# An RWKV attention with two feed-forwards on one core: the second feed-forward's weights split into device memory ahead of time, and all diagonal fills on ScalarE

## The chip, the core and the metric

The kernel runs on one core of a Trainium2 chip. Its engines work side by side, each through a list of its own, and wait for each other by semaphores: TensorE (matrix products into PSUM), VectorE, ScalarE, GpSimd, and SyncE, whose queue issues the transfers. The profile calls them PE, DVE, ACT, POOL and SP. The metric is the device time of one run in microseconds (us); lower is better.

## The reference

Three stages follow each other: a linear attention with a decaying state over 768 positions (4 batches, 8 heads of 48 channels), a feed-forward of 384 to 768 channels that takes the largest of three products, and a gated feed-forward of 384 to 1536 channels. All of it is in 32-bit floats.

```python
for t in range(S):
    cur = np.einsum('bhd,bhe->bhde', u[None] * kt, vt)
    y[:, :, t] = np.einsum('bhd,bhde->bhe', rt, state + cur)
    state = w[None, :, :, None] * state + np.einsum('bhd,bhe->bhde', kt, vt)
...
h = np.maximum(np.maximum(x @ w1, x @ w2), x @ w3)
x = h @ w_out
...
g = x @ w_gate
out = (g / (1 + np.exp(-g)) * (x @ w_val)) @ w_out
```

## The kernel before

**Units and blocks.** The 768 positions are cut into 6 blocks of 128. A block of one batch is a unit, so there are 24 units, four to a block. A unit loads its keys and queries (`qk`, 448 KB, L259) and its natural-order keys, values and receptances (`nat`, 576 KB, L260). GpSimd scales them: `qk` twice at L266, `nat` at L270, L271 and L275; for units 0 to 3 VectorE shares this work. TensorE forms the scores `s` (L297). VectorE sums the bonus `a0` (L280). The tile `am` gets the bonus on its diagonals by eight fills of 128x128 (`fill`, L286 on VectorE or L288 on ScalarE). Of units 0 to 2 each engine fills four; the later units are ScalarE's. VectorE then copies the scores into `am` under a mask (`select`, L300). TensorE multiplies for the unit's result `y` (L317 with the state, or L322, and L326 with `am`), and for the state's growth `u` (L345). ScalarE evacuates `y` into the block's `xr` (L334), GpSimd decays the state (L352), VectorE adds `u` (L359).

**First feed-forward.** Block i has six steps f. Each makes three products `m` (nine matmuls each), whose largest becomes `h`: ScalarE copies the first out of PSUM (L398), VectorE takes two maxima (L401). ScalarE rounds `h` to a high part (L405), GpSimd makes the low part (L408). Products `o` with the second weights follow. The units of block i+1 are done between the first steps of block i, so that TensorE's order alternates between some `m`, a unit's scores, more `m`, and the unit's result.

**Second feed-forward.** Block i has twelve steps: two products `g` each, a gate of both (ScalarE L426, VectorE L429), its split (L433, L408), and three accumulating products `oo`. The results leave by L445.

**Products and weights.** Each product of two 32-bit matrices is three matmuls of halves: high by high (L384), high by low (L385), low by high (L386). The weights arrive as 64-bit numbers, 384 KB for 128x384 of them. One such third of a weight tile is a job `k`; 18 jobs make the first up-projections (`w_a`), 6 its output (`w_b`) and 36 the second feed-forward (`w_c`). A job is a fetch (L191), a scaling on ScalarE (`t`, L196), three operations on VectorE in `top` (L213, L217, L210) and two in `rest` (L225, L227), the rounding to the high half on ScalarE (`put_hi`, L230), a conversion on ScalarE (`to_float`, L234), and a product for the low half (`put_lo`, L238) on GpSimd or VectorE. The 36 jobs of `w_c` write straight into their tiles. The first four of these tiles lie in memory that the attention uses until it is done, the others reuse tiles of the first feed-forward.

**What sets the order.** The kernel is planned as it is built. `Plan.run` knows every step with its engine, an assumed cost and what it needs, and always takes the step with the lowest rank: its earliest start less 0.08 times the length of what hangs on it. TensorE's order is written out by hand and given to the plan as `tensor_order`. Each engine then works through its own list in the order in which the plan placed the steps. The products `m`, `o` and `g` share four PSUM banks.

## Time and profile before

| what | value |
|---|---|
| median of three runs (lowest, highest) | 910.39 us (909.04, 910.5) |
| profiled execution, its span | 909.89 us, 908.2 us |
| PE busy | 865.2 us, 95% |
| DVE busy | 383.5 us, 42% |
| ACT busy | 323.4 us, 36% |
| POOL busy | 365.3 us, 40% |
| moved by DMA | 55.45 MB |

The shares are averages over the whole span. The busy time by stretch tells more: it is given for windows of the span, with the mean clock that TensorE was granted (1.00 is full) and the busy share of the DMA engines. In a timeline each row is one instruction, or several in a row of the same kind, with its start, its duration, its engine, line and tiles, and in brackets the time that its engine idled before it and what ended the wait. Rows of groups give the busy time of all instructions of one line and kind, and the mean duration of one in ns.

### The profile page before, as it was taken

What the parts mean: (1) busy time and instruction counts of PE and PEld (TensorE: products, weight loads), DVE (VectorE), ACT (ScalarE), POOL (GpSimd) and SP (SyncE); (2) the same over time, 40 slices, a digit from 0 to 9 for tenths busy, and PEclk for the clock granted to TensorE, in tenths of its full rate; (3) what the DMA queues carried; (4) which work ended last, traced back from release to release, by engine and by line L of the source; (5) the groups of instructions that cost most, each with busy time, mean ns of one, the idle gap of its engine ahead of it and who ended that gap; (6) DMA issues with size and microseconds to landing.
All of it is one profiled execution on the core that took longest, in us unless ns stands there. A gap on an engine that the chain in (4) does not pass through costs nothing.

```text
span 908.2 us, 12109 instructions
## 1 busy us (share of the span) xinstructions
PE 865.2 (95%) x4754; PEld 703.6 (77%) x4754; DVE 383.5 (42%) x615; ACT 323.4 (36%) x675; POOL 365.3 (40%) x322
## 2 busy tenths in 40 slices
PE   7869789999999999999998799999999999999998
PEld 6647668887887887888876578888888888888886
DVE  8999973333323322448999941121012012112101
ACT  3645644342242333325655542122222113122211
POOL 7575666644546635214444442222221222122221
PEclk8889889999999999999999999999999999999999
DMA  8335432323303302012434300000000000000000
GB/s 264 117 100 184 147 125 67 89 75 94 102 1 93 102 1 93 10 36 70 123 106 122 102 36 1 1 35 1 1 1 35 0 1 35 1 1 35 1 1 35
DMA packets 19323, 55.45 MB, mean 61 GB/s; under 512 B 2400, under 2 KB 3296, under 8 KB 19264
## 3 DMA queue, kind: packets, MB, share of 16 engines
q1 hardware_dynamic: 19264, 54.67, 19.6%
q8 instruction: 37, 0.61, 0.3%
q14 instruction: 22, 0.18, 0.1%
HBM read 48.96 MB, written 4.72 MB: 59 GB/s over the span
## 4 chain that ended last, share of the span: by engine, by line
PE 73%; DVE 17%; issue 3%; ACT 1%; DMA 1%; POOL 0%; DVEq 0%; ACTq 0%; POOLq 0%
PE g L386 9%; PE g L385 9%; PE g L384 9%; PE m L384 7%; PE m L386 6%; PE m L385 6%; PE oo L385 5%; PE oo L386 5%; PE oo L384 5%; DVE t L217 4%; DVE raw L225 3%; DVE t L213 2%; DVE raw L210 2%; PE o L386 2%; PE o L384 2%
## 5 line engine op out<-in xcount | busy, mean ns | idle before, releaser
L408 POOL TENSOR_TENSOR gs<-mm,gs 128x512 fp32r<-128x512 f32 x72 | 93.7, 1302 | 287.0 <-ACT gs L433 286.5
L384 PE MATMUL g<-xhi,w_c 128*128 128x512 f32 x432 | 169.5, 392 | 9.7 <-DVE mm L429 9.3
L429 DVE TENSOR_TENSOR mm<-mm,g 128x512 f32<-128x512 f32 x72 | 49.4, 687 | 300.2 <-PE g L386 299.1
L386 PE MATMUL g<-xhi,w_c 128*128 128x512 f32 x432 | 169.3, 392 | 0.9 <-POOL w_c L238 0.8
L385 PE MATMUL g<-xlo,w_c 128*128 128x512 f32 x432 | 168.7, 391 | 0.0
L384 PE MATMUL m<-xhi,w_a 128*128 128x512 f32 x324 | 133.5, 412 | 4.7 <-DVE h L401 4.7
L386 PE MATMUL m<-xhi,w_a 128*128 128x512 f32 x324 | 129.2, 399 | 2.6 <-DVE w_a L238 2.6
L385 PE MATMUL m<-xlo,w_a 128*128 128x512 f32 x324 | 128.7, 397 | 2.3 <-POOL xlo L379 1.4
L401 DVE TENSOR_TENSOR h<-h,m 128x512 f32<-128x512 f32 x72 | 49.3, 685 | 135.7 <-PE m L386 101.2
L384 PEld LDWEIGHTS g<-xhi,w_c 128*128 128x128 f32 x432 | 81.3, 188 | 29.8 <-DVE mm L429 6.1
L408 POOL TENSOR_TENSOR hs<-h,hs 128x512 fp32r<-128x512 f32 x36 | 54.7, 1519 | 103.3 <-ACT hs L405 103.2
L386 PEld LDWEIGHTS g<-xhi,w_c 128*128 128x128 f32 x432 | 81.4, 188 | 18.8 <-POOL w_c L238 1.9
L385 PEld LDWEIGHTS g<-xlo,w_c 128*128 128x128 f32 x432 | 81.4, 188 | 16.8
L433 ACT CAST gs<-mm 128x512 fp32r<-128x512 f32 x72 | 44.6, 620 | 139.3 <-DVE mm L429 139.3
L426 ACT ACTIVATE mm<-g 128x512 f32<-128x512 f32 x72 | 43.0, 597 | 136.9 <-PE g L386 136.9
L384 PE MATMUL oo<-gs,w_c 128*128 128x512 f32 x216 | 85.8, 397 | 0.7 <-ACT gs L433 0.7
L385 PE MATMUL oo<-gs,w_c 128*128 128x512 f32 x216 | 85.3, 395 | 0.9 <-POOL gs L408 0.9
L386 PE MATMUL oo<-gs,w_c 128*128 128x512 f32 x216 | 85.1, 394 | 0.0
L384 PEld LDWEIGHTS m<-xhi,w_a 128*128 128x128 f32 x324 | 62.2, 192 | 21.1 <-ACT w_b L230 3.3
L386 PEld LDWEIGHTS m<-xhi,w_a 128*128 128x128 f32 x324 | 62.2, 192 | 17.3 <-DVE w_a L238 3.5
L385 PEld LDWEIGHTS m<-xlo,w_a 128*128 128x128 f32 x324 | 62.4, 193 | 14.9 <-POOL xlo L379 1.7
L266 POOL TENSOR_TENSOR qk<-qk,P 112x512 f32<-112x512 f32 x43 | 57.0, 1343 | 26.9 <-DMA qk<-in_qk 26.9
(107 smaller groups left out, 1243.7 us busy)
## 6 DMA issues: line engine op xcount, KB each, us to landing
raw<-in_wup SPq DMA_DIRECT2D x54, 384.0 KB, 3.2
nat<-in_nat SPq DMA_DIRECT2D x22, 576.0 KB, 5.1
qk<-in_qk SPq DMA_DIRECT2D x24, 448.0 KB, 4.4
out<-ob SPq DMA_DIRECT2D x18, 256.0 KB, 2.1
raw<-in_wout SPq DMA_DIRECT2D x6, 384.0 KB, 3.3
xr<-xr SPq DMA_DIRECT2D x10, 96.0 KB, 3.0
kv<-in_nat SPq DMA_DIRECT2D x4, 192.0 KB, 9.5
r<-in_nat SPq DMA_DIRECT2D x2, 192.0 KB, 8.2
```

Source lines behind the costliest of these rows:

```text
L210: nc.vector.tensor_scalar(out=o, in0=hw, scalar1=0x1FF, scalar2=15, op0=ALU.bitwise_and, op1=ALU.logical_shift_left)
L217: nc.vector.scalar_tensor_tensor(out=t, in0=hw, scalar=0x80000000, in1=t, op0=ALU.bitwise_and, op1=ALU.bitwise_or)
L225: nc.vector.scalar_tensor_tensor(out=lw, in0=lw, scalar=17, in1=mid if k < nearly else hw, op0=ALU.logical_shift_right, op1=ALU.bitwise_or)
L266: eng.tensor_tensor(out=a, in0=a, in1=P[0:112], op=ALU.mult)
L384: nc.tensor.matmul(p, wh_, xh, start=first, stop=False)
L385: nc.tensor.matmul(p, wh_, xl, start=False, stop=False)
L386: nc.tensor.matmul(p, wl_, xh, start=False, stop=last)
L401: nc.vector.tensor_tensor(out=hs[i, f], in0=hs[i, f], in1=banks["m", i, f, j], op=ALU.max)
L408: eng.tensor_tensor(out=g[:, 1], in0=m, in1=g[:, 0].bitcast(F32), op=ALU.subtract)
L426: nc.scalar.activation(out=hs[i, f], in_=banks["g", i, f, 0], func=AF.Silu)
L429: nc.vector.tensor_tensor(out=hs[i, f], in0=hs[i, f], in1=banks["g", i, f, 1], op=ALU.mult)
L433: nc.scalar.copy(hsplit[i, f][:, 0], hs[i, f])
```

## The change

The second feed-forward's 36 jobs no longer write their halves into the tiles from which TensorE reads. Each splits its third in place, in a scratch tile with room for both halves, and a transfer (`put_away`) writes this to a tensor in device memory, `aside`. They are paced: job n of the 36 may be fetched only after a product `m` of block 1 + n // 9 of the first feed-forward, nine jobs to each of the blocks 1 to 4. In the plan's ranking these steps no longer count by what hangs on them, but by the head of TensorE's remaining order less 15 (`behind`). Twelve transfers of 1.18 MB (`bring`) then fetch the finished tiles back: five when the attention is closed, which now includes that all 36 jobs have been put away, the others as tiles of the first feed-forward come free. The pool for raw weights moves into the attention's part of the memory, and the pool for early tiles holds five instead of four. The fills of units 0 to 3 have only ScalarE to go to. The diff, cut to its core:

```diff
+EARLY = 5
...
-    def add(self, key, on, needs, do, lag=0.0, at=0.0):
+        self.behind = {}
+    def add(self, key, on, needs, do, lag=0.0, at=0.0, behind=None):
         self.steps[key] = (on, list(needs), do, lag, at)
+        if behind is not None:
+            self.behind[key] = behind
...
+        coming = self.tensor_order[::-1]
         while ready:
             best = None
+            while coming[-1] in done and len(coming) > 1:
+                coming.pop()
+            head = coming[-1]
             for k, options in ready.items():
                 for e, t in options:
                     start, cost = max(t, free[e]), steps[k][0][e]
                     shy = self.SPARE if e == "dve" and len(options) > 1 else 0.0
-                    rank = (start + shy - self.LOOK * rest[k], start + cost)
+                    weight = rest[k] if k not in self.behind else rest[head] - self.behind[k]
+                    rank = (start + shy - self.LOOK * weight, start + cost)
                     if best is None or rank < best[0]:
                         best = rank, k, e, start, cost
...
-    raw_p = pool(ctx, "raw", bufs=2)
...
+    raw_p = pool(att, "raw", bufs=2, side="right")
...
-    weights, raws, ts = {}, {}, {}
+    weights, raws, ts, parts = {}, {}, {}, {}
+    far = pool(ctx, "far", space=bass.MemoryType.DRAM)
+    aside = [far.tile([128, 2, 3, 384], F32, name=f"aside_{f}") for f in range(NF2)]
...
     def scale(k):
-        ts[k] = raw_p.tile([128, 384], U32, tag="t", name=f"t_{k}")
+        parts[k] = raw_p.tile([128, 2, 384], U32, tag="t", name=f"t_{k}")
+        ts[k] = parts[k][:, 0]
         nc.scalar.mul(ts[k].bitcast(F32), raws[k][:, :, 1].bitcast(F32), 2.0**-112)
     def part(k, q):
         key, z, _ = jobs[k]
+        if key[0] == "c":
+            return parts[k][:, q].bitcast(F32R)
         if key not in weights:
-            where = late["wp2"] if key[0] == "c" and key[1] < 4 else wpool
-            weights[key] = where.tile([128, 2, 3, 384], F32R, tag="w", name=f"w_{key[0]}{key[1]}")
+            weights[key] = wpool.tile([128, 2, 3, 384], F32R, tag="w", name=f"w_{key[0]}{key[1]}")
         return weights[key][:, q, z]
+    def put_away(k):
+        (_, f), z, _ = jobs[k]
+        nc.sync.dma_start(out=aside[f][:, :, z], in_=parts.pop(k).bitcast(F32))
+    def bring(f):
+        t = weights["c", f] = (late["wp2"] if f < EARLY else wpool).tile([128, 2, 3, 384], F32R, tag="w", name=f"w_c{f}")
+        nc.sync.dma_start(out=t.bitcast(F32), in_=aside[f])
...
             att.close()
-            late["wp2"] = pool(ctx, "wp2", bufs=4, side="right")
...
         for k, (key, z, _) in enumerate(jobs):
+            own, pace = {}, []
+            if key[0] == "c":
+                n = k - nearly
+                own, pace = {"behind": 15.0}, [("m", 1 + n // 9, 2 * (n % 9) // 3, 2 * (n % 9) % 3)]
             if k < 4:
                 add(("fetch", k), {"none": 0.0}, [], lambda e: None, at=17.5 + 1.1 * k)
             else:
-                add(("fetch", k), {"sync": 0.5}, [("lo", k - 4), ("branch",)], lambda e, k=k: fetch(k), lag=3.0)
-            room = []
+                add(("fetch", k), {"sync": 0.5}, [("lo", k - 4), ("branch",)] + pace, lambda e, k=k: fetch(k), lag=3.0, **own)
+            add(("scale", k), {"act": 0.42}, [("fetch", k)] + ([("hi", k - 2), ("rest", k - 2)] if k > 1 else [])
+                + ([("put", k - 2)] if k - 2 >= nearly else []),
+                lambda e, k=k: scale(k), **own)
+            add(("top", k), {"dve": 1.02 if k < nearly else 1.2}, [("scale", k)] + ([("rest", k - 1)] if k else []),
+                lambda e, k=k: top(k), **own)
+            add(("rest", k), {"dve": 0.74 if k < nearly else 0.86}, [("top", k)], lambda e, k=k: rest(k), **own)
+            add(("hi", k), {"act": 0.42}, [("top", k), ("rest", k)], lambda e, k=k: put_hi(k), **own)
+            add(("float", k), {"act": 0.42}, [("rest", k)], lambda e, k=k: to_float(k), **own)
+            add(("lo", k), {"pool": 1.14, "dve": 0.5}, [("float", k), ("hi", k)], lambda e, k=k: put_lo(k, engine[e]), **own)
             if key[0] == "c":
-                f = key[1] - 4
-                room = [("attention closed",)] if f < 0 else [("m", NB - 1, f, 2)] if f < NF1 else [("o", NB - 1, NK - 1, f - NF1)]
-            add(("scale", k), {"act": 0.42}, [("fetch", k)] + ([("hi", k - 2), ("rest", k - 2)] if k > 1 else []),
-                lambda e, k=k: scale(k))
-            add(("top", k), {"dve": 1.02 if k < nearly else 1.2}, [("scale", k)] + ([("rest", k - 1)] if k else []), lambda e, k=k: top(k))
-            add(("rest", k), {"dve": 0.74 if k < nearly else 0.86}, [("top", k)], lambda e, k=k: rest(k))
-            add(("hi", k), {"act": 0.42}, [("top", k), ("rest", k)] + room, lambda e, k=k: put_hi(k))
-            add(("float", k), {"act": 0.42}, [("rest", k)], lambda e, k=k: to_float(k))
-            add(("lo", k), {"pool": 1.14, "dve": 0.5}, [("float", k), ("hi", k)], lambda e, k=k: put_lo(k, engine[e]))
+                add(("put", k), {"sync": 0.5}, [("lo", k), ("hi", k)], lambda e, k=k: put_away(k), lag=3.0, **own)
+        for f in range(NF2):
+            q = f - EARLY
+            room = ("attention closed",) if q < 0 else ("m", NB - 1, q, 2) if q < NF1 else ("o", NB - 1, NK - 1, q - NF1)
+            add(("bring", f), {"sync": 0.5}, [room] + [("put", nearly + 3 * f + z) for z in range(3)],
+                lambda e, f=f: bring(f), lag=5.0)
         def weight(k):
-            return [("hi", k), ("lo", k)]
+            return [("bring", (k - nearly) // 3)] if k >= nearly else [("hi", k), ("lo", k)]
...
-                add(("fill", n, x), {"act": 1.2, "dve": 0.75} if first else {"act": 1.2}, [("a0", n)],
+                add(("fill", n, x), {"act": 1.2}, [("a0", n)],
                     lambda e, n=n, x=x: fill(n, x, engine[e]))
...
         add(("branch",), {"none": 0.0}, rows0 + [("flag",), ("u", B - 1)]
             + [("fill", n, x) for n in range(B) for x in range(2)], branch)
         add(("attention closed",), {"none": 0.0}, [("row", NB * B - 1), ("u", NB * B - 1)]
-            + [("update", n) for n in range((NB - 2) * B, (NB - 1) * B)], attention_closed)
+            + [("update", n) for n in range((NB - 2) * B, (NB - 1) * B)] + [("put", k) for k in range(nearly, len(jobs))],
+            attention_closed)
```

The lines of the new program stand 14 to 35 further down: L236, L240, L233, L248 and L250 are the five VectorE operations of a job, L303 is the bonus sum, L323 the select, L424 the maximum, L382 the state's sum, L311 the fill, L421 the copy of `h`, L428 its rounding, L357 the evacuation of `y`, L209, L253 and L257 the scaling, the rounding and the conversion of a job.

VectorE in block 2, from the select of unit 13 to that of unit 14 (`am_13` and `am_14` are the units' tiles, `h_2_2` the third step's maximum). Before:

```order
L300 COPY_PREDICATED am_13_1998<-mask_129,s0_13_2150 128x512
L300 COPY_PREDICATED am_13_1998<-mask_129,s1_13_2151 128x512
L280 TENSOR_REDUCE a0_14_2216<-nat_14_2135 128x8
L359 TENSOR_TENSOR st_1_132<-st_1_132,u_13_2196 112x192
L401 TENSOR_TENSOR h_2_2_2245<-h_2_2_2245,m_2_2_1_2205 128x512
L401 TENSOR_TENSOR h_2_2_2245<-h_2_2_2245,m_2_2_2_2233 128x512
L300 COPY_PREDICATED am_14_2217<-mask_129,s0_14_2247 128x512
L300 COPY_PREDICATED am_14_2217<-mask_129,s1_14_2248 128x512
```

After:

```order
L323 COPY_PREDICATED am_13_2126<-mask_143,s0_13_2302 128x512
L323 COPY_PREDICATED am_13_2126<-mask_143,s1_13_2303 128x512
L236 TENSOR_SCALAR t_35_2347<-t_35_2347 128x384
L240 SCALAR_TENSOR_TENSOR t_35_2347<-raw_35_2300,t_35_2347 128x384
L233 TENSOR_SCALAR raw_35_2300<-raw_35_2300 128x384
L248 SCALAR_TENSOR_TENSOR raw_35_2300<-raw_35_2300 128x384
L250 TENSOR_SCALAR raw_35_2300<-t_35_2347 128x384
L303 TENSOR_REDUCE a0_14_2379<-nat_14_2277 128x8
L382 TENSOR_TENSOR st_1_146<-st_1_146,u_13_2358 112x192
L424 TENSOR_TENSOR h_2_2_2408<-h_2_2_2408,m_2_2_1_2368 128x512
L424 TENSOR_TENSOR h_2_2_2408<-h_2_2_2408,m_2_2_2_2396 128x512
L323 COPY_PREDICATED am_14_2380<-mask_143,s0_14_2410 128x512
```

Job 35 now stands between the select of unit 13 and the bonus sum of unit 14; the other rows keep their order.

ScalarE at the same place, from the rounding `hs_2_1` of the second step's maximum past the fills of unit 14. Before:

```order
L405 CAST hs_2_1_2172<-h_2_1_2110 128x512
L334 COPY xr_3_2131<-y_13_2176 112x4x128
L288 ACTIVATE am_14_2217<-aeye_130,a0_14_2216 128x128 x8
L398 COPY h_2_2_2245<-m_2_2_0_2161 128x512
L405 CAST hs_2_2_2270<-h_2_2_2245 128x512
```

After:

```order
L428 CAST hs_2_1_2325<-h_2_1_2244 128x512
L209 ACTIVATE t_35_2347<-raw_35_2300 128x384
L253 CAST t_35_2347<-t_35_2347 128x384
L357 COPY xr_3_2273<-y_13_2329 112x4x128
L311 ACTIVATE am_14_2380<-aeye_144,a0_14_2379 128x128 x8
L421 COPY h_2_2_2408<-m_2_2_0_2314 128x512
```

The scaling and the rounding of job 35 now stand ahead of the evacuation of unit 13's `y` and of unit 14's fills.

VectorE at the start, from unit 0's bonus sum to the select of unit 1 (`nat_1` is unit 1's natural-order load, `qk_2` and `qk_3` the keys of units 2 and 3). Before:

```order
L280 TENSOR_REDUCE a0_0_221<-nat_0_101 128x8
L286 TENSOR_SCALAR am_0_222<-aeye_130,a0_0_221 128x128 x4
L300 COPY_PREDICATED am_0_222<-mask_129,s1_0_210 128x512
L300 COPY_PREDICATED am_0_222<-mask_129,s0_0_209 128x512
L266 TENSOR_TENSOR qk_2_109<-qk_2_109,P_159 112x512
L280 TENSOR_REDUCE a0_1_269<-nat_1_106 128x8
L286 TENSOR_SCALAR am_1_270<-aeye_130,a0_1_269 128x128 x4
L300 COPY_PREDICATED am_1_270<-mask_129,s1_1_243 128x512
L300 COPY_PREDICATED am_1_270<-mask_129,s0_1_242 128x512
```

After:

```order
L303 TENSOR_REDUCE a0_0_235<-nat_0_115 128x8
L293 TENSOR_TENSOR nat_1_120<-nat_1_120 128x384
L294 TENSOR_TENSOR nat_1_120<-nat_1_120,ub_111 128x384
L323 COPY_PREDICATED am_0_236<-mask_143,s0_0_223 128x512
L303 TENSOR_REDUCE a0_1_269<-nat_1_120 128x8
L323 COPY_PREDICATED am_0_236<-mask_143,s1_0_224 128x512
L289 TENSOR_TENSOR qk_2_123<-qk_2_123,P_173 112x512
L323 COPY_PREDICATED am_1_270<-mask_143,s0_1_252 128x512
L289 TENSOR_TENSOR qk_3_129<-qk_3_129,P_173 112x512
L323 COPY_PREDICATED am_1_270<-mask_143,s1_1_253 128x512
```

The fills are gone, the two products on `nat_1` have come over from GpSimd, and the scaling of unit 3's keys has moved up.

## Rows read from the trace of the kernel before

**Rows 1.** Busy us by stretch: start:end, length, PE, PEld, DVE, ACT, POOL, clock, DMA, GB/s

```profile
59.00:97.00 38.00, 28.33 (x207) 21.58 (x207) 36.63 (x55) 22.43 (x55) 24.98 (x23) 0.86 0.44 139
...
200.40:265.50 65.10, 65.10 (x473) 52.84 (x472) 21.52 (x31) 21.97 (x54) 34.60 (x31) 1.00 0.23 69
393.90:442.80 48.90, 48.90 (x217) 40.53 (x216) 36.63 (x60) 24.00 (x49) 18.88 (x17) 1.00 0.28 76
442.80:537.00 94.20, 82.09 (x325) 63.27 (x324) 84.49 (x141) 53.28 (x106) 44.20 (x39) 0.95 0.33 95
...
537.00:610.40 73.40, 73.40 (x325) 60.79 (x324) 11.31 (x16) 17.47 (x29) 16.70 (x13) 1.00 0.03 11
```

**Rows 2.** Timeline of the start: VectorE's and ScalarE's fills (start, length, instruction)

```profile
12.42 3.74 DVE L286 TENSOR_SCALAR am<-aeye,a 128x128 f32<-128x128 f32 x4
...
17.50 1.31 DVE L266 TENSOR_TENSOR qk<-qk,P 112x512 f32<-112x512 f32 x1
...
19.31 2.79 DVE L286 TENSOR_SCALAR am<-aeye,a 128x128 f32<-128x128 f32 x4
...
25.90 1.68 DVE L286 TENSOR_SCALAR am<-aeye,a 128x128 f32<-128x128 f32 x4
...
28.58 2.45 ACT L288 ACTIVATE am<-aeye,a 128x128 f32<-128x128 f32 x8 [0.80 <-DVE a L280]
```

**Rows 3.** Timeline of one unit step in block 2, engine by engine

```profile
215.99 2.53 POOL L266 TENSOR_TENSOR qk<-qk,P 112x512 f32<-112x512 f32 x2 [4.32 <-DMA qk<-in_qk]
...
222.24 1.00 POOL L275 TENSOR_TENSOR nat<-nat,PT 128x384 f32<-128x384 f32 x1
...
217.97 1.37 DVE L300 COPY_PREDICATED am<-mask,s 128x512 f32<-128x512 uint8 x2 [0.40 <-PE s L297]
...
225.73 0.69 DVE L401 TENSOR_TENSOR h<-h,m 128x512 f32<-128x512 f32 x1 [2.57 <-ACT h L398]
...
228.12 1.36 DVE L300 COPY_PREDICATED am<-mask,s 128x512 f32<-128x512 uint8 x2 [0.40 <-PE s L297]
...
222.29 0.59 ACT L334 COPY xr<-y 112x512 f32<-112x512 f32 x1 [4.07 <-PE y L326]
222.77 2.46 ACT L288 ACTIVATE am<-aeye,a 128x128 f32<-128x128 f32 x8
...
231.30 1.09 PE L326 MATMUL y<-am,nat 128*64 128x128 f32 x16
```

**Rows 4.** Groups of VectorE by line, 59 to 97 us (busy, mean ns, idle before)

```profile
L225 DVE SCALAR_TENSOR_TENSOR raw<-raw,x 128x384 uint32<-128x384 uint32 x8 | 6.7, 836 | 0.0
L217 DVE SCALAR_TENSOR_TENSOR t<-raw,t 128x384 uint32<-128x384 uint32 x7 | 6.5, 934 | 0.0
L227 DVE TENSOR_SCALAR raw<-t 128x384 uint32<-128x384 uint32 x8 | 6.3, 793 | 0.0
L213 DVE TENSOR_SCALAR t<-t 128x384 uint32<-128x384 uint32 x7 | 5.0, 709 | 1.4 <-ACT t L196 1.4
L210 DVE TENSOR_SCALAR x<-raw 128x384 uint32<-128x384 uint32 x7 | 4.7, 669 | 0.0
```

**Rows 5.** The same view, 200 to 393 us

```profile
L225 DVE SCALAR_TENSOR_TENSOR raw<-raw 128x384 uint32<-128x384 uint32 x2 | 1.1, 560 | 0.1
...
L210 DVE TENSOR_SCALAR raw<-raw 128x384 uint32<-128x384 uint32 x2 | 0.7, 362 | 0.1
```

**Rows 6.** Timeline of VectorE beside GpSimd in block 0

```profile
60.03 1.44 DVE L227 TENSOR_SCALAR raw<-t 128x384 uint32<-128x384 uint32 x1
...
59.65 2.95 POOL L266 TENSOR_TENSOR qk<-qk,P 112x512 f32<-112x512 f32 x2
```

**Rows 7.** Transfers: 137 to 330 us, then the first 22 us (count, size, us to landing)

```profile
qk<-in_qk SPq DMA_DIRECT2D x12, 448.0 KB, 3.9
...
DMA packets 2523, 5.98 MB, mean 272 GB/s; under 512 B 412, under 2 KB 1308, under 8 KB 2522
...
qk<-in_qk SPq DMA_DIRECT2D x4, 448.0 KB, 8.8
```

More of the change, by code (lines that the diff above doesn't have):

```diff
@@ L546, in attention_closed @@
             att.close()
-            late["wp2"] = pool(ctx, "wp2", bufs=4, side="right")
+            late["wp2"] = pool(ctx, "wp2", bufs=EARLY, side="right")
         order = [(q, n) for q, n in zip("ssyuyussyuyu", (0, 1, 0, 0, 1, 1, 2, 3, 2, 2, 3, 3))]
```

## The prediction

> **What bounds the kernel now.** I read the busy time by stretch first [rows 1], since the page's shares are averages over very different stages. The reader should see three things in it. From 59 to 97 us, inside the first block of the first feed-forward, VectorE is busy for 36.63 of 38.00 us and TensorE for 28.33: VectorE, which splits the first weights, sets the pace there. In the block from 200.40 to 265.50 TensorE is busy for all 65.10 us and VectorE for 21.52: TensorE sets the pace, at a granted clock of 1.00. The block from 442.80 to 537.00 is the first of the second feed-forward. It takes 94.20 us, and the next one, with the same 325 matmuls, takes 73.40. In the long one VectorE is busy for 84.49 us, because it splits that phase's weights one step ahead of their use.
>
> Of its extra 20.80 us, 8.69 are TensorE's own (82.09 busy against 73.40, at a granted clock of 0.95), and the other 12.11 are waits. So a microsecond of waiting here came with another 0.7 us of slower matmuls.
>
> **What the change takes away.** With the splits of the 36 jobs moved forward, the block from 442.80 should run like the one after it: 94.20 - 73.40 = **20.80 us less**. What is next late there would be the weights' way back. Five tiles of 1.18 MB are asked for as the last block of the first feed-forward begins, and that block lasts 48.90 us [rows 1]. At the 272 GB/s that the queue moved in the first 22 us [rows 7] they take 5.9 / 0.272 = 22 us, so they fit, and the later tiles are each wanted one step of about 6 us (73.40 / 12) after another. I put their cost at nothing. If they got half that rate the five would take 43 us, which still fits.
>
> **The head.** VectorE's twelve fills go, in groups of four that took 3.74, 2.79 and 1.68 us [rows 2], each beside four on ScalarE. After the change ScalarE does all eight of a unit, which took it 2.45 us for unit 3 [rows 2]. By size alone that is 1.29 + 0.34 - 0.77 = 0.9 us sooner. VectorE can also do the next unit's scaling and sums, 1.81 us from 17.50 to 19.31 [rows 2], while ScalarE fills; once or twice that is hidden, so 2.7 or 4.5 us. Against it, two products of unit 1 come over from GpSimd's list, and TensorE's warm-up matmuls stand ahead of the first result. The ends are 0 and 4.5; I take **2.8 us less**, near the case of one overlap. The gain is kept, because block 0 is bound by VectorE, whose list there keeps its order.
>
> **What comes in: nine split jobs in each of blocks 1 to 4.** In volume everything fits under TensorE. A job is five VectorE operations: two of two inputs at 0.56 us and three of one at 0.36 when nothing disturbs them [rows 5], so 2.2 us, and nine add 20 us to 21.52 of 65.10. GpSimd gets at most nine products of about 1 us on 34.60. ScalarE gets three operations per job. What matters is therefore the order, and how long one job really holds VectorE.
>
> The loop to watch is this one [rows 3]. A select ends at 217.97 + 1.37 = 219.34. In the new order a whole job follows it on VectorE, and ScalarE's list has the rounding of that job ahead of the evacuation of the unit's result and of the next unit's fills. So the fill now starts no sooner than 219.34 + J + 2 x 0.48 us (the evacuation held up the fill by 0.48, and I charge the rounding the same). From the fill to the first maximum 2.96 us pass (222.77 to 225.73), two maxima take 1.38, the select 1.36. Loop: J + 6.66 us. The units follow each other every 10.15 us (217.97 to 228.12), and TensorE wants the selected tile at 231.30, 1.82 us after the select's end. Two steps of each block run through the whole loop (units 13 to 14 and 14 to 15 in this block), so TensorE is held for 2 x (J + 6.66 - 10.15) - 1.82 = **2J - 8.8 us** per block. Up to J = 4.4 this costs nothing. The step before them has two jobs but no fill in its way, and I count it as fitting.
>
> How long is J? The lower end is 2.2 us. In the stretch 59 to 97 the five operations averaged 0.84, 0.93, 0.79, 0.71 and 0.67 us [rows 4], together 3.94, with GpSimd busy for 24.98 of 38.00 us [rows 1], a share of 0.66. In the unit steps of blocks 1 to 3 its share is higher: it works without a gap from 215.99, where the next unit's keys are scaled, to the end of its last product at 223.24 [rows 3]. What such a run does to VectorE stands in [rows 6]: GpSimd's pair of products from 59.65 lasts 2.95 us (2.53 in the steady block), and beside it VectorE's one-input operation of 60.03 takes 1.44 us instead of 0.36. It starts during one GpSimd operation and ends only after it, at 61.47, 0.35 us after half of the pair. So a job that starts at 219.34 gets one operation through per GpSimd operation until about 224.0 (223.24, and 0.2 us for each of four lengthened operations), and its last one after that: J of about 5.5 us by count, and 6.9 if every operation took 1.4. The row with a comparable share says 3.94. I take 5.2, nearer to the count, since the placement right behind the select puts the job under that run.
>
> The Trainium skill speaks to this row: its page "SBUF — State Buffer", section "Who interferes with whom", says that VectorE (in its two-port modes, or with two inputs from SBUF) and GpSimd share one pair of ports as an exclusive lock, and that whoever starts first keeps it for a whole instruction. The row at 60.03 agrees, but an average of 3.94 over 38 us shows that a job is not always caught. By the rule alone this change would move 36 jobs from a stretch where GpSimd is half idle under one where it is not; the second rival below works that out.
>
> At J = 5.2 the loop costs 1.6 us per block. After the block's last select two jobs stand ahead of the maxima of the fifth step, which free TensorE's banks. They take about 5.2 + 3 us, against some 7 that TensorE can go on with the banks it has, so I add 1.3. That makes 2.9 us in each of three blocks and about 1 in the fourth, where GpSimd has only two units left to prepare: 9.6 us. TensorE's slower matmuls after a wait come on top. By the first block of the second feed-forward they are 0.7 per us, and nothing if the waits stay short; I take half: 3.4. Together **13 us more**, with ends of 0 (J up to 4.4) and about 37 (J = 6.7, by the same sum: 4.6 and 2.1 per block, 3.3 blocks, times 1.7).
>
> **Transfers and queues.** Loads of the units land after 3.9 us for the keys in the steady blocks [rows 7]. The jobs add 28 MB in blocks 1 to 4, some 109 GB/s over 258 us to the 69 of [rows 1], together well under the 272 of the start. On the queue of SyncE the write of one job waits for GpSimd's last product of it and stands ahead of a later unit's loads; that product should be done some 6 us before those loads can be asked for. A new wait is that of a job's scaling on ScalarE: its scratch tile must have been written out by the transfer of two jobs earlier, and in the step shown this scaling stands ahead of the rounding, the evacuation and the fills. That transfer is issued behind the unit's two loads, whose first lands at 215.99 [rows 3] and so left about 3.9 us earlier [rows 7], at 212.1. Put at 213.5, and at the 3.9 us of that somewhat larger load, the transfer is done by 217.4, and the scaling is due before the select's end at 219.34, so about 2 us are spare. Cost: nothing, with the rival of late transfers for the case that either isn't so.
>
> **The sum.** The profiled execution took 909.89 us. 909.89 - 20.80 - 2.8 + 13 = 899.3. The median of the runs shown, 910.39, is 0.5 longer, so I give **900 us**.
>
> **Rivals.**
> The jobs fit: J stays at 2.2 to 4.4, as the average of [rows 4] says, and TensorE never waits. 909.89 - 20.80 - 2.8 + 0.5 = 887 us, 886 to 891 with the ends of the head. For it speaks that GpSimd stops whenever TensorE does, so the run of operations doesn't last. Against it is the place of the job. Chance 0.30.
>
> The loop takes over as the bound, and the kernel is slower than before: every operation of a job is held as in [rows 6], J is 6.7 and the waits of 2 us and more bring the slower clock with them. 37 us more than nothing: 924 us, from 912 to 930. It decides against the change once the added waits exceed 20.80 + 2.8 = 23.6 us, which by the sum above is at J of about 6.2. The rule of the page "SBUF — State Buffer" of the Trainium skill would lead here. For this rival speak [rows 6], against it [rows 4]. Chance 0.18.
>
> Transfers come late: the keys took 8.8 us to land in the busy first 22 us [rows 7], 4.9 more than in the blocks. If the new traffic did half of that, the 2 us to spare ahead of the scaling would just do; if it did all of it, some 2 us at each of the 9 or 10 places where a job stands ahead of fills come on top of the forecast's 13: about 918, from 912 to 922. Chance 0.05.
>
> The weights come back late, or the last write does, so that part of the 20.80 us stays: half of it gives 910, no change. Chance 0.04.
>
> **Chances and range.** Forecast (891 to 908) 0.43, and the rivals as above. Leaving out about 0.05 below and 0.13 above, the range is 886 to 914. A measurement of this kernel can tell about 0.2%, 1.8 us, from no change. Faster: 0.43 + 0.30, less a little for the forecast's upper end, 0.71. Same: 0.08. Slower: 0.21.
>
> **What would show it.** In the changed kernel's trace: the first block of the second feed-forward lasts 73 to 74 us with TensorE busy throughout; the first up-projection starts about 3 us sooner; in blocks 1 to 3 TensorE waits for VectorE's selects and maxima, 2 to 4 us per block, with J between 4.5 and 5.5 behind the selects, and granted clocks slightly below 1.00. If J is under 4.4 there and TensorE is always busy, the first rival is right. If blocks 1 to 3 last over 73 us, the second is. If TensorE or GpSimd waits for a load, the third is. I am wrong altogether if the block after 442 us keeps its length.

## The result: 921.18 us, 1.2% slower

The changed kernel takes 921.18 us (median of 4 runs, 918.67 to 921.67) against 909.71 us before (4 runs). The ratio is 1.0123, with a 95% interval of 1.0098 to 1.0147: slower, and outside the range that was given.

The stretches of the changed kernel, cut where TensorE starts a new block (columns as in [rows 1]): block 0 of the first feed-forward, its blocks 1 to 5, and the first block of the second.

```profile
31.60:134.28 102.68, 79.46 (x475) 60.33 (x474) 88.40 (x145) 54.65 (x124) 65.80 (x57) 0.88 0.48 148
134.28:209.54 75.26, 69.86 (x474) 55.27 (x473) 55.07 (x72) 34.38 (x85) 50.31 (x44) 0.95 0.41 133
209.54:284.28 74.74, 69.84 (x474) 55.18 (x473) 57.62 (x78) 34.22 (x82) 45.54 (x39) 0.95 0.47 154
284.28:357.66 73.38, 68.20 (x473) 53.94 (x472) 57.38 (x77) 32.44 (x79) 43.22 (x38) 0.98 0.49 157
357.66:425.42 67.76, 65.27 (x409) 51.80 (x408) 48.30 (x74) 34.33 (x79) 30.25 (x27) 0.97 0.43 140
425.42:474.38 48.96, 48.96 (x217) 40.54 (x216) 12.51 (x19) 11.64 (x21) 10.28 (x8) 1.00 0.76 306
474.38:548.00 73.62, 73.62 (x326) 60.98 (x325) 11.33 (x15) 18.75 (x30) 16.69 (x13) 1.00 0.00 1
```

The last row stands where [rows 1] has 94.20 us: it takes 73.62 now, with TensorE busy throughout at a granted clock of 1.00. So the change does what it is for, and takes 20.6 us away. The four rows in the middle are the price. Before, these blocks took 65.10, 65.09, 65.10 and 63.28 us; now they take 75.26, 74.74, 73.38 and 67.76, together 32.6 us more. Block 5 is as it was (48.96), at 306 GB/s of weights coming back. The kernel before, blocks 1, 3 and 4 (block 2 is in [rows 1]):

```profile
135.31:200.41 65.10, 65.10 (x474) 52.84 (x472) 22.73 (x34) 26.44 (x70) 41.92 (x39) 1.00 0.26 81
...
265.50:330.60 65.10, 65.10 (x474) 52.84 (x473) 20.66 (x31) 22.07 (x54) 34.68 (x31) 1.00 0.23 68
330.60:393.88 63.28, 63.28 (x410) 50.56 (x409) 23.27 (x35) 18.40 (x40) 21.32 (x17) 1.00 0.12 37
```

Each of the four rows holds two losses, as the prediction's first part showed for [rows 1]. Length less PE busy is the waits: 5.4, 4.9, 5.2 and 2.5 us, together 18.0. PE busy less the old length of the block is the same matmuls at a lower clock: 4.8, 4.8, 3.1 and 2.0, together 14.6. The granted clock is 0.95 to 0.98 where it was 1.00.

What TensorE waits for there, the three largest (us in total, times, longest):

```profile
PE y L349 <- ACT hs L428: 9.2, 7, 2.2
PE o L408 <- POOL hs L431: 5.1, 3, 1.9
PE y L349 <- DVE am L323: 1.8, 7, 0.3
```

The releasers are ScalarE, GpSimd and VectorE by turns, so this view alone names no culprit. The step that the prediction followed, two units later in the trace, does. VectorE, ScalarE, GpSimd and TensorE in block 2, from the select of unit 13:

```profile
227.09 1.36 DVE L323 COPY_PREDICATED am<-mask,s 128x512 f32<-128x512 uint8 x2 [0.40 <-PE s L320]
229.94 0.74 DVE L236 TENSOR_SCALAR t<-t 128x384 uint32<-128x384 uint32 x1 [1.48 <-ACT t L209]
230.71 1.51 DVE L240 SCALAR_TENSOR_TENSOR t<-raw,t 128x384 uint32<-128x384 uint32 x1
232.26 1.53 DVE L233 TENSOR_SCALAR raw<-raw 128x384 uint32<-128x384 uint32 x1
233.82 0.56 DVE L248 SCALAR_TENSOR_TENSOR raw<-raw 128x384 uint32<-128x384 uint32 x1
234.41 0.36 DVE L250 TENSOR_SCALAR raw<-t 128x384 uint32<-128x384 uint32 x1
234.69 0.55 DVE L303 TENSOR_REDUCE a<-nat 128x8 f32<-128x384 f32 x1
...
238.66 1.48 DVE L424 TENSOR_TENSOR h<-h,m 128x512 f32<-128x512 f32 x2 [3.16 <-ACT h L421]
240.06 1.34 DVE L323 COPY_PREDICATED am<-mask,s 128x512 f32<-128x512 uint8 x2
...
229.36 0.55 ACT L209 ACTIVATE t<-raw 128x384 f32<-128x384 f32 x1 [2.01 <-DMA raw<-in_wup]
...
235.71 2.45 ACT L311 ACTIVATE am<-aeye,a 128x128 f32<-128x128 f32 x8
...
230.42 1.39 POOL L431 TENSOR_TENSOR hs<-h,hs 128x512 fp32r<-128x512 f32 x1
...
232.56 1.02 POOL L298 TENSOR_TENSOR nat<-nat,PT 128x384 f32<-128x384 f32 x1
...
253.27 0.40 PE L349 MATMUL y<-am,nat 128*64 128x128 f32 x2 [1.63 <-ACT hs L428]
```

The select ends at 228.45. The job (five rows, 229.94 to 234.77) comes before the bonus sum at 234.69, the sum before the fills at 235.71, the fills before the maxima at 238.66, these before the select at 240.06: the loop that [rows 3] closed in 10.15 us takes 12.97. The next turn takes 12.38 (240.06 to 252.44), and at 253.27 TensorE has waited for 1.63 us. The row names ScalarE's `hs`, but `y` needs the unit's two selects and not `hs`. They run from 252.44 at 0.67 us each, so the first is through at about 253.1; the rest of `y` then waits another 0.25 us, which the profile does put down to the select. The two-input operation of 230.71 takes 1.51 us and the one-input one of 232.26 1.53, where [rows 5] has 0.56 and 0.36. Their ends, 232.22 and 233.79, lie 0.41 and 0.21 us behind the ends of GpSimd's `hs` (231.81) and of its last product on `nat` (233.58). With GpSimd through, the next two take 0.56 and 0.36.

The same five operations over blocks 1 to 4, with two other groups of VectorE (busy, mean ns):

```profile
L240 DVE SCALAR_TENSOR_TENSOR t<-raw,t 128x384 uint32<-128x384 uint32 x34 | 32.5, 957 | 1.2
L233 DVE TENSOR_SCALAR raw<-raw 128x384 uint32<-128x384 uint32 x34 | 29.4, 866 | 1.2
L248 DVE SCALAR_TENSOR_TENSOR raw<-raw 128x384 uint32<-128x384 uint32 x34 | 29.1, 856 | 0.9
L236 DVE TENSOR_SCALAR t<-t 128x384 uint32<-128x384 uint32 x35 | 22.1, 632 | 16.0 <-ACT t L209 15.9
L323 DVE COPY_PREDICATED am<-mask,s 128x512 f32<-128x512 uint8 x32 | 21.6, 727 | 2.4 <-PE s L320 2.4
L250 DVE TENSOR_SCALAR raw<-t 128x384 uint32<-128x384 uint32 x34 | 20.4, 600 | 1.2
...
L303 DVE TENSOR_REDUCE a<-nat 128x8 f32<-128x384 f32 x15 | 8.1, 542 | 0.0
```

A job averages 3.91 us, as it did in [rows 4]. The select (0.73) and the sum (0.54) last what they lasted in block 0 of the kernel before (0.72 and 0.54, from 59 to 97 us); the job's operations are held, these two are not.

At the start, the chain of waits of the changed kernel (start, length) and that of the kernel before have one long piece each:

```profile
36.44 7.83 DMA raw<-in_wup
```

```profile
41.07 5.82 DMA raw<-in_wup
```

The first up-projection starts at 31.60 instead of 36.22, 4.6 us sooner, but the first fetch of weights after it, behind the units' loads, ends at 44.27 instead of 46.89, 2.6 us sooner. Block 0 ends 1.0 us sooner (134.28, before 135.31). The whole account: 32.6 - 20.6 - 1.0 = 11.0 us; the medians say 11.5.

### The profile page after: what moved, and what is told of

Same layout as the page of the kernel before. It is cut to its first block, busy times and chain, and to the rows that moved or that the text cites. A ratio compares the mean times of both kernels' runs of the same rounds, so it can differ in the third digit from the quotient of the medians.

```text
span 919.0 us, 12194 instructions
## 1 busy us (share of the span) xinstructions
PE 869.3 (95%) x4758; PEld 705.7 (77%) x4758; DVE 410.7 (45%) x607; ACT 326.8 (36%) x687; POOL 368.0 (40%) x318
## 4 chain that ended last, share of the span: by engine, by line
PE 61%; DVE 18%; DMA 6%; ACT 6%; issue 4%; POOL 1%; SPq 0%; DVEq 0%; ACTq 0%; POOLq 0%
PE g L408 11%; PE g L407 11%; PE g L409 11%; DMA raw<-in_wup 6%; PE oo L408 5%; PE oo L407 5%; PE oo L409 5%; DVE t L240 3%; ACT am L311 3%; PE m L407 3%; PE m L409 3%; PE m L408 3%; DVE raw L250 2%; DVE raw L248 2%; DVE raw L233 2%
## 5 line engine op out<-in xcount | busy, mean ns | idle before, releaser
L407 PE MATMUL oo<-gs,w_c 128*128 128x512 f32 x216 | 84.0, 389 | 0.0
L408 PE MATMUL oo<-gs,w_c 128*128 128x512 f32 x216 | 84.0, 389 | 0.0
L409 PE MATMUL oo<-gs,w_c 128*128 128x512 f32 x216 | 84.0, 389 | 0.0
L424 DVE TENSOR_TENSOR h<-h,m 128x512 f32<-128x512 f32 x72 | 49.2, 683 | 69.7 <-PE m L409 36.4
L431 POOL TENSOR_TENSOR hs<-h,hs 128x512 fp32r<-128x512 f32 x36 | 57.1, 1587 | 49.7 <-ACT hs L428 49.6
L311 ACT ACTIVATE am<-aeye,a 128x128 f32<-128x128 f32 x192 | 59.2, 390 | 22.3 <-DVE a L303 21.3
```

The lines of the kernel that those rows point to most:

```text
L311: eng.mul(o, aeye, f)
L407: nc.tensor.matmul(p, wh_, xh, start=first, stop=False)
L408: nc.tensor.matmul(p, wh_, xl, start=False, stop=False)
L409: nc.tensor.matmul(p, wl_, xh, start=False, stop=last)
L424: nc.vector.tensor_tensor(out=hs[i, f], in0=hs[i, f], in1=banks["m", i, f, j], op=ALU.max)
L431: eng.tensor_tensor(out=g[:, 1], in0=m, in1=g[:, 0].bitcast(F32), op=ALU.subtract)
```

## The experiments

**One part alone.** First the fills without the jobs, from the kernel before:

```diff
-    add(("fill", n, x), {"act": 1.2, "dve": 0.75} if first else {"act": 1.2}, [("a0", n)],
+    add(("fill", n, x), {"act": 1.2}, [("a0", n)],
```

> The kernel before, with only the second part of the change: all fills of units 0 to 3 on ScalarE. In the changed kernel's trace the first up-projection starts 4.6 us sooner (31.60 instead of 36.22) but block 0 ends only 1.0 us sooner (134.28 instead of 135.31), since the first weight fetch after the start, asked for 4.6 us sooner, lands only 2.6 us sooner beside the units' loads, and the rest goes at the end of the block. Theory: the head's gain is mostly lost in block 0, so 908 to 909, 1 us less than before. Rival (the gain is lost only because of what the other part of the change does): 905 to 906.

907.72 us against 910.53, ratio 0.9967 (0.9952 to 0.9983), so 2.8 us. In its trace block 0 starts at 31.56 and ends at 133.85, 1.5 us sooner than before; a little more comes in the first block of the second feed-forward. Most of the head's 4.6 us is lost in block 0 without the jobs too. The median is 0.3 us below the theory's range.

Then the jobs without the fills, the reverse of that diff on the changed kernel:

> The changed kernel without its second part: the fills of units 0 to 2 are shared by VectorE and ScalarE as before. The fills alone gave 2.8 us. Theory (the two parts add up): block 0 ends near 135.3 as before, blocks 1 to 4 keep their lengths of 75, 75, 73 and 68 us, the total is 921 to 924. Rival (the earlier start disturbs the jobs of blocks 1 to 4): blocks 1 to 4 shorter by over 1 us each, the total under 918.

923.11 us, ratio to the kernel before 1.0123 (1.0096 to 1.0151). Blocks 1 to 4 take 75.87, 73.56, 74.40 and 66.68 us. So the jobs alone lose as much as the whole change, within the noise (a gain of 2.8 us by the fills can't be told in the difference): the loss belongs to the jobs.

**The jobs' operations cut to 16 columns.**

```diff
+        if k >= nearly:
+            t, hw = t[:, 0:16], hw[:, 0:16]
```

> The changed kernel, with the five VectorE operations of each of the 36 jobs of the second feed-forward cut to 16 of 384 columns (the rest of these weights is left unsplit); every engine's list keeps its order, all transfers and ScalarE's and GpSimd's operations stay whole. Theory (the length of a job on VectorE, ahead of the fills, makes the loop too long, and the slower clock follows the waits): blocks 1 to 3 go back from 75.3, 74.7 and 73.4 us to about 65, block 4 from 67.8 to 63.5, the total to 887 to 891. Rival 1 (late transfers hold ScalarE's scaling, and the list behind it): half of the 32.6 us stays, 900 to 908. Rival 2 (ScalarE's three operations per job are what delays the fills): over 900 as well, with ScalarE named in TensorE's waits.

898.62 us, and blocks of 69.10, 68.06, 67.77 and 63.54 us: 9.9 of the 32.6 us stay, between the theory's line and the first rival's, and both have a part. The jobs are shorter, 2.05 us on average, but their operations are still held. The rows of one job, the longest behind a select in this block, with GpSimd's beside them (128x16 instead of 128x384):

```profile
241.11 0.87 DVE L238 TENSOR_SCALAR t<-t 128x16 uint32<-128x16 uint32 x1
242.01 1.19 DVE L242 SCALAR_TENSOR_TENSOR t<-raw,t 128x16 uint32<-128x16 uint32 x1
243.24 1.21 DVE L235 TENSOR_SCALAR raw<-raw 128x16 uint32<-128x16 uint32 x1
244.48 0.93 DVE L252 SCALAR_TENSOR_TENSOR raw<-raw 128x16 uint32<-128x16 uint32 x1
245.45 0.18 DVE L254 TENSOR_SCALAR raw<-t 128x16 uint32<-128x16 uint32 x1
...
240.68 1.27 POOL L435 TENSOR_TENSOR hs<-h,hs 128x512 fp32r<-128x512 f32 x1 [0.44 <-ACT hs L432]
241.90 2.52 POOL L293 TENSOR_TENSOR qk<-qk,P 112x512 f32<-112x512 f32 x2
244.38 1.00 POOL L297 TENSOR_TENSOR nat<-nat 128x384 f32<-128x384 f32 x1
```

Five operations on 16 columns take 4.5 us, from 241.11 to 245.63. The last runs undisturbed in 0.18; the others take 0.87 to 1.21, each ending 0.03 us behind an operation of GpSimd (the halves of its pair end at about 243.16 and 244.42). With all 384 columns they ended 0.41 and 0.21 us behind one. So how long these four last is set by when GpSimd's operation ends, and their own size only adds what comes behind it. That is the held operation of [rows 6] in its plainest form.

The two jobs that stand in the loop take 2.9 us (221.35 to 224.24) and 3.7 (230.82 to 234.53) here, instead of 4.83 and 5.86. The turns take 11.43 and 10.30 us, and TensorE's unit products hardly wait any more (0.2 us in blocks 1 to 4). What waits is the output product, for GpSimd's low part: 6.0 us, one wait of 2.0 in each of blocks 1 to 3. Ahead of each of them ScalarE's list had stood for a fetch of weights, for 6.12, 6.61 and 6.77 us, and this is the first rival's part. The one of block 2, with `hs` on ScalarE at 260.79 and GpSimd's low part at 262.19 behind it:

```profile
259.82 0.55 ACT L209 ACTIVATE t<-raw 128x384 f32<-128x384 f32 x1 [6.61 <-DMA raw<-in_wup]
...
263.96 0.50 PE L412 MATMUL o<-hs,w_b 128*128 128x512 f32 x1 [2.01 <-POOL hs L435]
```

**GpSimd's preparing operations cut to 16 columns**, VectorE's jobs whole:

```diff
+        if n >= 2 * B:
+            a, p = a[:, 0, 0:16], p[:, 0, 0:16]
+            ...
+            ku, rk, u_ = ku[:, 0, 0:16], rk[:, 0, 0:16], ub[:, 0, 0:16]
```

> The changed kernel, with GpSimd's five preparing operations of units 8 to 23 (keys and queries twice, the bonus twice, the decayed keys) cut to 16 columns, so that most of the attention's input is left unscaled; every list keeps its order, and VectorE's jobs are whole. Theory (a job is long because VectorE is held by GpSimd's operations): a job behind a select falls from 4.8 to 6.3 us to under 3.2, blocks 1 to 3 to 65 to 67 us, the total to 888 to 896. Rival (VectorE's list has too much in it whatever GpSimd does, or transfers are late): jobs stay above 4 us or blocks above 70, the total above 907.

891.44 us. A job averages 2.88 us; the two of the loop in block 2 take 2.6 and 3.6, the second over the 3.2 that was expected, and the turns 10.92 and 10.16. Blocks 1 to 4 take 66.45, 65.61, 66.22 and 63.98. The first two in the view by stretch:

```profile
133.70:200.20 66.50, 65.44 (x474) 52.77 (x473) 43.90 (x71) 32.87 (x82) 26.65 (x41) 1.00 0.47 150
200.20:265.80 65.60, 65.38 (x474) 52.74 (x473) 46.92 (x77) 34.01 (x82) 27.54 (x39) 1.00 0.55 176
```

GpSimd is busy for 27 instead of 46 to 50 us, VectorE for 44 to 47 instead of 55 to 58 with the same operations, and the clock is back at 1.00. 28.9 of the 32.6 us are gone, as the theory had it. The two gains, 22.7 and 28.9 us, are more than the 32.6 together: a job is in the way by its own length and by the time for which it is held, and taking either away brings the loop most of the way back to 10.15 us.

**Both cuts.** 

> The changed kernel with both cuts at once: the five VectorE operations of the 36 jobs (as in e2_narrow_vector) and GpSimd's five preparing operations of units 8 to 23 (as in e3_narrow_gpsimd) work on 16 columns only, so both weights and attention input are left mostly unprocessed. All transfers, ScalarE's part and every list's order are whole. What is left of the added time is then the transfers and ScalarE's three operations per job. Theory (neither costs anything by itself): blocks 1 to 4 at 65.1, 65.1, 65.1 and 63.3 us within 0.5 us, the total 885 to 890. Rival (late transfers hold ScalarE and with it the fills): blocks 1 to 3 still at 66.5 us or more, the total above 893.

886.97 us. Blocks 1 to 4 take 65.09, 65.09, 65.10 and 63.28, and TensorE waits for nothing in them. Block 2:

```profile
197.81:262.90 65.09, 65.09 (x473) 52.83 (x472) 32.34 (x75) 32.80 (x78) 23.45 (x39) 1.00 0.52 173
```

Transfers and ScalarE's part of the jobs, all whole here, cost nothing by themselves. ScalarE still stands for the fetch ahead of the output product, 3.87 us in block 2, and the two fetches there take 8.4 us to land, as with the jobs alone cut; but TensorE is not held by it. They are asked for 46.8 us into the block, with the jobs alone cut 50.9 and in the changed kernel 57.0. So it is mostly the delay from the loop that makes this fetch come too late.

**Every third written twice.**

```diff
         nc.sync.dma_start(out=aside[f][:, :, z], in_=p)
+        nc.sync.dma_start(out=again[f][:, :, z], in_=p)
```

> The changed kernel, with each job's split third written to device memory twice, to two tensors (14 MB more over blocks 1 to 4, 36 transfers more on SyncE's queue). Theory (the transfers take little part): the landing of a weight fetch in blocks 1 to 4 grows from 5.2 us by under 1.5 us, blocks 1 to 3 by under 2 us each, the total 921 to 926. Rival (the added transfers are a main part of the loss): blocks 1 to 3 grow by 4 us or more each, the total above 932.

928.12 us, between the two. The landing of a weight fetch grew only from 5.5 to 6.0 us, but blocks 1 to 3 took 78.46, 76.21 and 77.13, 3.2, 1.5 and 3.8 us more. With the loop already too long, a transfer that comes later lengthens it: ScalarE's scaling waited 11.2 us for a scratch tile's writing, before the doubling 6.9, and 30.2 us for fetches, before 21.0. So the transfers are no cause of their own (both cuts), but they add to a loop that has no slack.

**The job moved behind the sum.** The third and fourth of each nine jobs get two needs more:

```diff
+    unit = B * (n // 9 + 2) + n % 9 if n % 9 in (2, 3) else None
...
-    add(("top", k), ..., [("scale", k)] + ([("rest", k - 1)] if k else []),
+    add(("top", k), ..., [("scale", k)] + ([("rest", k - 1)] if k else []) + ([("a0", unit)] if filled else []),
...
+    add(("hi", k), {"act": 0.42}, [("top", k), ("rest", k)] + filled, ...
```

> The changed kernel, with one more need for the third and fourth of each nine jobs: their VectorE operations may start only after the bonus sum of the unit whose fills follow, and their rounding on ScalarE only after those fills, so that neither stands ahead of the fills any more. The jobs still run beside GpSimd, at 4.8 to 6.3 us each. Theory (the place in the loop turns the held operations into waits): the step goes back to 10.15 us for these two, TensorE's waits at the unit's product go, blocks 1 to 3 take 66 to 69 us, the total is 893 to 902. Rival (VectorE and GpSimd together have too much to do for any order): blocks 1 to 3 stay above 72 us, the total above 912.

906.87 us, ratio to the kernel before 0.9945 (0.9927 to 0.9963): a gain of 14 us on the change, but less than the theory had, and blocks of 67.05, 72.02, 70.57 and 67.74. Where the sum waits now, on ScalarE and VectorE in block 2:

```profile
226.85 0.56 ACT L209 ACTIVATE t<-raw 128x384 f32<-128x384 f32 x1 [2.78 <-DMA raw<-in_wup]
...
227.71 0.55 ACT L257 ACTIVATE raw<-raw 128x384 f32<-128x384 uint32 x1
...
228.29 1.15 DVE L261 TENSOR_TENSOR t<-raw 128x384 fp32r<-128x384 f32 x1 [1.86 <-ACT raw L257]
...
239.64 0.55 DVE L303 TENSOR_REDUCE a<-nat 128x8 f32<-128x384 f32 x1 [4.02 <-POOL nat L294]
```

At 226.85 ScalarE's scaling has waited for a fetch of weights, and the conversion at 227.71 behind it. On VectorE the low half of another job stood ahead of the sum (229.36), and waited 1.86 us for that conversion. At 239.64 the sum waited 4.02 us for GpSimd's product. Taking the job out of the one place leaves the two engines as crowded as before. The expectation that this place alone was worth 20 us or more fell.

**The preparing moved to VectorE**, which did such operations in 0.69 and 0.56 us at the start when undisturbed (one beside GpSimd took 1.31, at 17.50 in [rows 2]), where GpSimd needs 1.27 and 1.00 ([rows 3]):

```diff
-    add(("scaled", n, q), both if first else one, [("load", n)],
+    add(("scaled", n, q), both if first else {"dve": 0.69}, [("load", n)],
...
-    {"dve": 1.0, "pool": 1.95} if first else {"pool": 1.95}
+    {"dve": 1.0, "pool": 1.95} if first else {"dve": 1.1}
```

With the needs of the run before:

> As e5_behind_sum, and four of GpSimd's five preparing operations of each unit from the fifth on (the scaling of keys and queries, the two bonus products; together 4.6 us) moved to VectorE, where such operations took 0.69 and 0.56 us at the start, 2.5 us per unit. Theory (what is scarce is the time in which the two engines may work at all, so moving work to the one that is faster at it helps): a job takes under 3.5 us, blocks 1 to 3 take 65.1 to 67 us, the total is 887 to 895. Rival (VectorE becomes the bound, with 20 us more of jobs, 10 of preparing and 21 of its own in 65): blocks 1 to 3 above 69 us, the total above 902.

880.55 us, ratio to the kernel before 0.9653 (0.9631 to 0.9676). Blocks 1 to 4 take 65.09, 65.09, 65.10 and 63.27 us, a job 2.90, and block 0 falls to 94.13, so that the total is below the theory's range. To part this from the change, the same move on the kernel before, and on the changed kernel without the needs:

> The kernel before with one thing of e6_prep_on_vector alone: four of the five preparing operations of each unit from the fifth on moved from GpSimd to VectorE; weights and fills as before. Question: how much of the 30 us that e6 gained has nothing to do with the change. Theory: block 0, where both engines are busy, gets 4 to 6 us shorter (99.1 to about 94), blocks 1 to 4 keep 65.1 and 63.3, the first block of the second feed-forward keeps its 94, the total is 904 to 907. Rival (the moved operations do not help where VectorE sets the pace): 910 or more.

903.75 us against 909.79, ratio 0.9933 (0.9901 to 0.9965). Block 0 takes 94.70 instead of 99.09, blocks 1 to 4 are as before; a fifth of what the run before gained.

> The changed kernel with the preparing operations moved to VectorE as in e6_prep_on_vector, but without the added needs of e5_behind_sum. The bonus sum still stands ahead of the job on VectorE here, since the preparing operations that it needs are on the same engine. Theory (the shared ports are what mattered, the added needs hardly): within 3 us of e6_prep_on_vector, 878 to 884, blocks 1 to 3 at 65 to 66 us. Rival (the needs carry a good part): above 887, blocks above 67 us.

879.31 us, ratio 0.9667 (0.9621 to 0.9713). The needs were not needed as such: with the preparing on VectorE, the sum stands ahead of the job in the loop in any case, as the expectation says. By stretch (block 0, block 2, the first block of the second feed-forward):

```profile
31.60:123.40 91.80, 77.11 (x475) 59.46 (x474) 89.35 (x163) 55.49 (x129) 49.30 (x41) 0.89 0.54 166
...
188.50:253.60 65.10, 65.10 (x474) 52.84 (x473) 56.64 (x92) 34.60 (x81) 25.97 (x24) 1.00 0.53 175
...
431.10:504.60 73.50, 73.50 (x326) 60.89 (x325) 11.24 (x15) 18.75 (x30) 16.70 (x13) 1.00 0.00 1
```

In block 2 VectorE is busy for 56.64 us, as in the changed kernel, with 10 us more to do; GpSimd for 25.97. A job takes 3.06 us on average, for 3.91. This kernel beats both, and on top of the moved preparing (903.75) the change is worth 24.4 us by the medians. Between the two profiled runs it is 27.3: 7.5 at the end of block 0 (123.36 for 130.86), and the 20 us of the second feed-forward.

## Why the prediction was wrong

**What bounds the kernel; what goes.** Right. The first block of the second feed-forward now takes 73.62 us; 20.80 less was said, 20.6 came. The weights' way back costs nothing.

**The head.** The first product starts 4.6 us sooner, the upper end given. The reason why it would be kept failed: block 0 is not bound by VectorE's list alone, and the first fetch, asked for 4.6 us sooner behind the same loads, landed 2.6 us sooner. In the changed kernel 1.0 us is left at the end of block 0, for 2.8.

**The jobs in blocks 1 to 4.** This is the step that failed, by its sizes; the mechanism, a held job in the loop, was right. 13 us were forecast, 32.6 came: 18.0 of waits for 9.6, and 14.6 of slower matmuls for 3.4.
- J was taken at 5.2 us; the two jobs of the loop in block 2 took 4.83 (229.94 to 234.77) and 5.86. That term holds, and so does its reason: with GpSimd's preparing cut the two take 2.6 and 3.6 us, and with VectorE's own operations cut to a 24th they still take 2.9 and 3.7, where five undisturbed ones of 0.18 make 0.9.
- The job was assumed to start at the select's end. It started 1.49 us later, since ScalarE's scaling waited for the weights (229.36, 2.01 us for the fetch). I had asked whether the scratch tile would be free in time, and not whether the fetch itself would have landed. In blocks 1 to 3 the unit's products waited 2.5 to 3.0 us, for the 1.6 that was said.
- The end of the block was put at the maxima, 1.3 us. In blocks 1 to 3 the wait was at the output product, 2.2 to 2.3 us, and the forecast had no transfer there. In block 2 ScalarE's list stands 4.22 us for a fetch of weights (4.26 and 4.41 in blocks 1 and 3), the rounding `hs` of a maximum that was done at 273.59 comes behind it, and GpSimd's low part behind that:

```profile
273.90 0.55 ACT L209 ACTIVATE t<-raw 128x384 f32<-128x384 f32 x1 [4.22 <-DMA raw<-in_wup]
...
274.87 0.62 ACT L428 CAST hs<-h 128x512 fp32r<-128x512 f32 x1
...
276.53 1.39 POOL L431 TENSOR_TENSOR hs<-h,hs 128x512 fp32r<-128x512 f32 x1
...
277.97 0.50 PE L408 MATMUL o<-hs,w_b 128*128 128x512 f32 x1 [1.93 <-POOL hs L431]
```

  The fetch is asked for at 266.53, behind the transfers of `xr`, the two loads of a unit and two thirds that are written out, and lands 7.3 us later.
- In the sum of volumes I gave GpSimd nine products of 1 us; that VectorE's jobs would slow its other work was left out. It slows them less than they slow the jobs: `hs` takes 1.27 us alone (253.26), 1.39 and 1.61 beside a job (230.42 and 245.34). By estimate, block 2's 45.54 us less the 34.60 of [rows 1] and the eight products of 0.83 that GpSimd had there leave 4.3 us. The longest `hs`, 2.98 at 266.09, starts beside VectorE's copy of `xr` (265.66 to 267.68), which is no part of a job; such a one took 2.22 in the kernel before (248.76).
- Block 4 was put at 1 us of waits and had 2.5.
- The lower clock was put at 0.35 us per us of waiting, half of what the first block of the second feed-forward showed, on the argument that the waits would be short. It came to 14.6 / 18.0 = 0.81. The row that was there, 0.72, was the better guide, and halving it had no row behind it. With it, the 9.6 us alone would have given 16.5.

**The rivals.** The second one came true, slower with the loop as the bound, at 921 in its 912 to 930. Its reason needed J of 6.2 or more; with 0.72 us of slower matmuls per us of waiting the same sum needs about 5.7. J was 5.3 on average in block 2, and the rest came from the late fetches, in the loop and ahead of the output product, and from the clock. It had 0.18. The Trainium skill's rule (page "SBUF — State Buffer", section "Who interferes with whom"), that VectorE and GpSimd hold a shared pair of ports for whole instructions, pointed there. The rows with 16 columns agree with it. So does the sum, a reduction, which that section says never contends, at 0.54 us throughout. I had set an average of 3.94 us against the rule; the average is the same in the changed kernel (3.91) and says nothing of the jobs that stand in the loop.

**The third rival**, late transfers, holds 921 in its 912 to 922 as well. Its sign, TensorE or GpSimd waiting for a load, did not come, but ScalarE's scaling waited 21.0 us for fetches and 7.2 for scratch tiles over blocks 1 to 4, which I had put at nothing. With both cuts the transfers alone cost nothing.

**The first rival** (the jobs fit) is what happens once GpSimd has less to do: 879 to 891 us in the four kernels in which its preparing was cut or moved.

**Not settled.** No run brings the fetches in time and leaves the jobs held, so how much of the 32.6 us hangs on the late fetches is not known; the rows give them 1.5 us in the loop of block 2 and a part in 5.1 us of waits at the output products. Nor was it tried whether the same waits in other places would slow the matmuls as much (14.6 us); in the runs without the waits the granted clock is 1.00 again.

## What to carry to other kernels

Before work is moved behind another engine's bound stage, ask whether VectorE and GpSimd will both run there, and count operations, not only bytes: each VectorE operation of this kind that met a busy GpSimd cost the rest of GpSimd's operation (up to 1.53 us for one of 0.36), and lengthened GpSimd's by a little (1.27 to 1.61). Moving work of the one onto the other, where it is faster, can relieve both, even when that engine looks the busier one, as it did here. In a loop across engines, check the landing of every transfer that its first operation waits for, and price a wait of TensorE with the slower matmuls behind it, from a row of the same kernel.

## What was not expected of the hardware

An integer operation of VectorE on 128x16 elements, 0.18 us when undisturbed, took up to 1.21 us beside GpSimd in the job shown (and 1.39 at 222.21), hardly less than the longest on 128x384, 1.53. And VectorE with 10 us more work per block was busy no longer than before (56.64 us, in the changed kernel 57.62), while GpSimd had 20 us less and held the jobs less (3.06 us for 3.91).
